# Turning the decayed k with VectorE and SBUF transfers in a gated-linear-attention and SiLU kernel

## The chip, the cores and the metric

The kernel runs on one core of a Trainium2 chip. The metric is the device time of one execution in microseconds (us), lower being better; it is the median of several runs. The core has five engines which work side by side, each through its own list of instructions: TensorE (PE in the profile; its weight loads are the row PEld), VectorE (DVE), ScalarE (ACT), GpSimd (POOL) and SyncE (SP), which here only issues transfers.

## The reference

Two blocks follow each other. Shapes: 4 batches, 8 heads, 768 tokens, 48 columns per head; then 3072 tokens of 384 columns through a hidden layer of 2048.

```python
def _attn_ref(q, k, v, alpha):
    state = np.zeros((B, H, D, D), dtype=np.float32)
    for t in range(S):
        state = alpha[:, :, t, :, None] * state + np.einsum('bhd,bhe->bhde', k[:, :, t], v[:, :, t])
        y[:, :, t] = np.einsum('bhd,bhde->bhe', q[:, :, t], state)
    return y

def _moe_ref(x, w_in, w_out):
    h = x @ w_in
    g = h * (1.0 / (1.0 + np.exp(-h)))
    return g @ w_out
```

Between them the heads are laid side by side, (B, H, S, D) to (B*S, H*D). The weights come as 64-bit floats, the rest as 32-bit floats.

## The kernel before, in words

The sequence is cut into 6 blocks of 128 tokens. A *chunk* n is one block of one batch, with all 8 heads: 24 chunks, the four batches of a block after each other (`ci, b = divmod(n, B)`). Heads lie in pairs: a tile of 128 partitions and 4 x 128 columns holds 4 pairs, each pair in two halves of 64 partitions of which 48 are used.

Within a chunk the recurrence is written with products of the decay. For each chunk there are five stages:

- `products(n)` takes the products of alpha backward over the chunk with a scan (L699), and multiplies k by them: `kp` (L713, L715). Up to chunk 7 (`NA` = 8) the inputs are brought to "column on partition" by TensorE transposes (L694); from chunk 8 on they are loaded in quads and turned by VectorE in blocks of 32x32 (`turned`, L674). From chunk 8 on, the two halves of 64 tokens of the heads of the second two pairs are swapped in `kp`.
- `quotient(n)` makes the forward products with a second scan (L728) and multiplies q by them (L733): `qp`.
- `scores(n)` multiplies `kp` with `qp` on TensorE (L757) into two PSUM banks, u = 0 and 1 for the two heads of a pair. Only the earlier tokens may count for a later one, so the result is masked: up to chunk 3 by a ScalarE copy and a GpSimd select (L763, L764), from chunk 4 on by a VectorE multiplication with a mask tile (L768). The masked scores are `g`. From chunk 8 on, the blocks of the scores that are zero anyway are not computed; `blank(n)` has ScalarE write zeros to the two banks ahead of time (L741). Then `kp` is transposed by TensorE (L774) and copied by ScalarE to `kn` (L776), with tokens on partitions; the last block of each batch (chunks 20 to 23) needs no `kn`. ScalarE also multiplies the state by the chunk's whole decay (L780).
- `values(n)` multiplies `g` with v, and the state with `qp`, on TensorE (L800) and copies the sum into `xt` (L805), the input of the second block.
- `states(n)` multiplies `kn` with v (L815) and adds that to the state on VectorE (L821), and after it v of chunk n+2 is loaded.

The second block works on groups of four chunks. Groups 0 and 1 multiply `xt` with `w_in` plainly (L858). The later ones save products by sums of blocks: `enter` (L882), with sums and differences on VectorE (L896) and copies and SiLU on ScalarE (L888, L893). `leave` multiplies with `w_out` in halves (L980), with subtractions on VectorE (L985) and stores of the result (L994, L996). The 64-bit weights are rounded to 32 bits on the way in: ScalarE takes the low part (L609, `rounding`), VectorE does the rest (L623 to L625); `convert` starts a piece at a time. In the second half an audit reads inputs again and VectorE reduces them (L663).

The order of the work is set on two levels. The loop over steps writes it: in step s, slot 0 has scores(s-1), slot 1 products(s), slot 2 values(s-1) and states(s-1), and slot 3, from step 8 on, quotient(s) and blank(s); `fill` puts pieces of the second block between the slots as their due times come. On this program the tile framework then works: it holds buffers in pools, adds the waits, and its planner may list instructions of an engine in another order than the one written, except where `keep_in_program_order` forbids it. On the chip each engine follows its list. The pool `ps_a` has three PSUM banks for scores, values, states and transposes; `kn`, `kp`, `qp` and `g` have one buffer each in the late steps. Nearly all transfers are issued on the sync queue, in the order of its list.

The change touches `scores`, `values`, `states` and `weights`, and puts `flip` in the place of `blank`:

Of the kernel before, what the change touches and what calls it, by code (L numbers as in the profile page):

```python
# [355 lines left out]
def quotients(  # L356
# [172 lines left out]

    mask = consts.tile([128, 2, C], F32, name="mask")  # L530
    gps.memset(mask, 1.0)
    for odd in range(2):
        for e in range(2):
            m = mask[CH * e : CH * e + CH, odd, :]
            gps.affine_select(m, m, pattern=[[1, C]], compare_op=ALU.is_ge, fill=0.0,
                              base=-CH * (e ^ odd), channel_multiplier=-1)

# [56 lines left out]
    def weights(which):  # L594
# [18 lines left out]
        for i, (dst, src) in enumerate(pieces):  # L613
            if not wide:
                act.dma_start(dst, src)
                yield
                continue
            assert which == 0 or conv_done[0] == n_conv[0]
            bits = coming.pop(0)
            up = ahead.pop() if ahead else rounding(bits)  # L620
            hi, w = bits[:, :, 1], dst.bitcast(I32)
            tc.keep_in_program_order(
                dve.tensor_scalar(w, hi, 3, 0x3FFFFFFF, ALU.logical_shift_left, ALU.bitwise_and))  # L623
            dve.scalar_tensor_tensor(w, hi, -(1 << 30), w, ALU.bitwise_and, ALU.bitwise_or)
            dve.tensor_tensor(w, w, up, ALU.add)  # L625
            if i + 1 < len(pieces):
                ahead.append(rounding(coming[0]))
            fetch()
            yield
# [104 lines left out]

    def blank(n):

        if n < NA:
            return
        ps = ctxs[n]["blank"] = [ps_attn() for _ in range(2)]
        for t in ps:  # L740
            act.activation(t.rearrange("p j c -> p (j c)"), ident[:, 0:1].to_broadcast([128, 4 * C]),  # L741
                           AF.Copy, scale=0.0)

    def scores(n):
        c = ctxs[n]
        ci, b = c["ci"], c["b"]
        ps = c.pop("blank") if n >= NA else [ps_attn() for _ in range(2)]

        for j in (0, 2, 1, 3):
            for e in range(2 if n >= NA else 1):
                for u in range(2):
# [4 lines left out]
                              start=True, stop=True)  # L758
        g = c["g"] = work.tile([128, 2, NP, C], F32, name="g")
        for u in range(2):  # L760
            if n < GB:

                act.copy(g[:, u], ps[u])  # L763
                gps.affine_select(g[:, u], g[:, u], pattern=[[0, NP], [1, C]], compare_op=ALU.is_ge,  # L764
                                  fill=0.0, base=0, channel_multiplier=-1)
                continue
            m = mask[:, :, None, :] if n >= NA else mask[:, 0:1, None, :]
            dve.tensor_tensor(g[:, u].rearrange("p (o j) c -> p o j c", o=2),  # L768
                              ps[u].rearrange("p (o j) c -> p o j c", o=2),
                              m.to_broadcast([128, 2, NP // 2, C]), ALU.mult)  # L770
        if ci < NCH - 1:
            ps_k = ps_attn()
            for j in range(NP):
                pe.transpose(ps_k[:, j, :], c["kp"][:, j, :], ident)  # L774
            c["kn"] = work.tile([128, NP, C], F32, name="kn")
            act.copy(c["kn"], ps_k)  # L776
# [8 lines left out]
    def values(n):  # L785

        c = ctxs[n]
        ci, b, g, qp = c["ci"], c["b"], c["g"], c["qp"]
        vn = c["v"].rearrange("p (j u) d -> p j (u d)", u=2)
        s = st[b].rearrange("p j u e -> p j (u e)")  # L790
        py = ps_attn()
        todo = [(3 * j + i, vn[:, j, at : at + 32], g[:, u, j, :])
                for j in range(NP) for i, at, u in ((0, 0, 0), (1, 32, 0), (2, 80, 1))]
        todo += [(3 * j + 1, vn[:, j, 48:80], g[:, 1, j, :]) for j in range(NP)]
        if ci > 0:
# [10 lines left out]
    def states(n):  # L806
        c = ctxs.pop(n)
        ci, b, vn = c["ci"], c["b"], c["v"]
        if ci < NCH - 1:

            ps = ps_attn()
            for j in range(NP):
                for i in range(4):
                    r = slice(32 * i, 32 * i + 32)
                    pe.matmul(ps[r, j, 0:D], lhsT=c["kn"][:, j, r], rhs=vn[:, 2 * j + i // 2, 0:D],  # L815
                              start=True, stop=True)
# [288 lines left out]
    def settle():  # L1105

        first.close()
        late.update(look=pool("look"), part=pool("part"), xc=pool("xc"), turn=pool("turn"),
                    wx=pool("wx").tile([128, 8, NQ, 128], F32, name="wx"))
        quads = pool("quads")  # L1110
# [5 lines left out]
    def fill(step, slot):  # L1116

        at = step * SLOTS + slot
        if at < marks[0]:
            if step >= 1:  # L1120
                convert(0, (at - SLOTS) * 3 // (marks[0] - SLOTS) + 1)
# [11 lines left out]
    for step in range(STEPS):  # L1133
# [6 lines left out]
        elif step >= NA:  # L1140
            stages = [[(scores, 1)], [(products, 0)], [(values, 1), (states, 1)], [(quotient, 0), (blank, 0)]]
        for slot, group in enumerate(stages):
            for stage, lag in group:
# [10 lines left out]
                if stage is states and n + NV < NT:  # L1154
                    load_v(n + NV)
            fill(step, slot)
            if step * SLOTS + slot >= NA * SLOTS - 1 and conv_done[1] == NFT and not late:
# [21 lines left out]
    ps = ps_attn()[0:1, 0, 0:1]  # L1179
    pe.matmul(ps, lhsT=good, rhs=mask[:, 0, C - 1 : C], start=True, stop=True)  # L1180
    dve.tensor_single_scalar(small, ps, 127.5, ALU.is_ge)
# [62 lines left out]
```

## Time and profile before

| | |
|---|---|
| time, median of 3 runs | 563.47 us (563.33 to 563.66) |
| span of the profiled execution | 561.6 us |
| busy PE, PEld | 543.9 us, 492.6 us |
| busy VectorE, ScalarE, GpSimd | 453.0, 205.3, 15.1 us |
| TensorE transposes of `kp`, L774 | 80 |
| ScalarE: blanks L741, copies of `kn` L776 | 32 of 0.598 us, 20 of 0.584 us |
| VectorE: masks L768 | 40 of 0.685 us |
| GpSimd: selects L764 | 8 of 0.865 us |

A line of groups gives the source line, engine, operation, output and inputs by name and shape, the count, the busy time and the mean duration of one. A fp32 matmul leaves two records, a transpose one, so the count of PE records is above that of the instructions. The slices cut the span in 40 and show the busy share of each in tenths. The chain is followed back from the last instruction to what released it, step by step, so it tells which engines' work set the end. Records of matmuls overlap, since they are pipelined: the distance between starts says what one costs, and their ends are modelled.

### The profile page before, as it was taken

How to read it: one execution, taken by the hardware profiler on the slowest of the kernel's cores; microseconds unless marked ns; L12 is line 12 of the kernel's file. 1: busy time of each engine (PE TensorE's matmuls, PEld its weight loads, DVE VectorE, ACT ScalarE, POOL GpSimd, SP SyncE). 2: the span in 40 equal slices, each digit the busy share in tenths (PEclk: the TensorE clock that was granted, in tenths of full speed). 3: DMA queues.
4: the chain of work that ended last, by engine and by line, in shares of the span. 5: the costliest groups of instructions: out<-in, count | busy, mean ns of one | idle time of the engine just before them, and what ended most of it. 6: DMA issues, size and time to landing. Idle time of an engine off the chain costs nothing.

```text
span 561.6 us, 12420 instructions
## 1 busy us (share of the span) xinstructions
PE 543.9 (97%) x5074; PEld 492.6 (88%) x5074; DVE 453.0 (81%) x829; ACT 205.3 (37%) x406; POOL 15.1 (3%) x36
## 2 busy tenths in 40 slices
PE   5899999999999999999999999999999999999996
PEld 3688887998999999899989999999998999899995
DVE  5797899966999799986998897899895875857731
ACT  2566543213233342443433443434443342332100
POOL 4211000100000000000000000000000000000000
PEclk9899999999999999999999999999999999999998
DMA  9989971143443333333425544435522123334200
GB/s 206 230 241 223 234 183 34 43 126 100 100 107 89 73 97 87 101 87 85 131 70 160 142 108 134 130 81 153 136 69 81 53 85 118 99 94 125 71 30 26
DMA packets 94417, 63.81 MB, mean 114 GB/s; under 512 B 55312, under 2 KB 86032, under 8 KB 94352
## 3 DMA queue, kind: packets, MB, share of 16 engines
q1 hardware_dynamic: 94352, 62.94, 43.3%
q8 instruction: 41, 0.67, 0.5%
q14 instruction: 24, 0.20, 0.1%
HBM read 58.20 MB, written 4.72 MB: 112 GB/s over the span
## 4 chain that ended last, share of the span: by engine, by line
PE 75%; DVE 14%; DMA 5%; SPq 2%; issue 2%; ACT 1%; POOL 0%; DVEq 0%; ACTq 0%
PE ps_o L980 33%; PE ps_m L882 18%; PE ps_m L858 11%; PE ps_a L800 6%; DMA bits<-in_moe_w_out_dram 3%; PE ps_a L757 3%; DVE seen L663 2%; PE ps_a L774 1%; DVE g L896 1%; DMA bits<-in_moe_w_in_dram 1%; DVE u L699 1%; PE ps_a L815 1%; DVE w_out L625 1%; DVE p L728 1%; SPq L456 1%
## 5 line engine op out<-in xcount | busy, mean ns | idle before, releaser
L980 PE MATMUL ps_o<-w_out,g 128*128 128x192 f32 x768 | 133.6, 328 | 1.1 <-DVE o L994 1.1
L980 PEld LDWEIGHTS ps_o<-w_out,g 128*128 128x128 f32 x768 | 125.5, 190 | 3.9 <-DVE o L994 1.5
L980 PE MATMUL ps_o<-wt,g 128*128 128x192 f32 x576 | 100.0, 327 | 0.0
L980 PEld LDWEIGHTS ps_o<-wt,g 128*128 128x128 f32 x576 | 95.1, 190 | 1.5
L858 PE MATMUL ps_m<-xt,w_in 128*128 128x256 f32 x384 | 88.5, 382 | 1.0 <-ACT xt L805 1.0
L858 PEld LDWEIGHTS ps_m<-xt,w_in 128*128 128x128 f32 x384 | 71.0, 190 | 11.0 <-ACT xt L805 1.4
L882 PE MATMUL ps_m<-xc,w_in 128*128 128x256 f32 x288 | 70.1, 379 | 0.0
L882 PEld LDWEIGHTS ps_m<-xc,w_in 128*128 128x128 f32 x288 | 54.0, 190 | 6.4 <-DVE g L896 0.2
L663 DVE TENSOR_REDUCE seen<-bits 128x1 f32<-128x384 int32 (+2 forms) x65 | 42.4, 689 | 16.8 <-DMA bits<-in_moe_w_out_dram 16.5
L893 ACT ACTIVATE g<-g 128x1024 f32<-128x1024 f32 x32 | 33.1, 1055 | 57.5 <-DVE g L896 57.5
L985 DVE TENSOR_TENSOR g<-g 128x512 f32<-128x512 f32 x72 | 48.5, 686 | 5.6 <-PE ps_o L980 5.6
L882 PE MATMUL ps_m<-xc,wx 128*128 128x256 f32 x192 | 50.1, 383 | 0.0
L888 ACT COPY g<-ps_m 128x512 f32<-128x512 f32 x64 | 36.8, 587 | 36.1 <-PE ps_m L882 36.0
L780 ACT ACTIVATE st<-st,least 128x96 f32<-128x96 f32 x80 | 24.1, 364 | 58.4 <-DVE least L702 58.4
L882 PEld LDWEIGHTS ps_m<-xc,wx 128*128 128x128 f32 x192 | 35.0, 190 | 4.2 <-issue 0.4
L896 DVE TENSOR_TENSOR g<-ps_m,g 128x512 f32<-128x512 f32 x56 | 37.4, 683 | 0.8 <-PE ps_m L882 0.5
L699 DVE TENSOR_TENSOR_SCAN u<-al,one 128x516 f32<-128x516 f32 x24 | 29.1, 1212 | 10.4 <-ACT al L696 10.3
L728 DVE TENSOR_TENSOR_SCAN p<-al,inv 128x516 f32<-128x516 f32 x24 | 29.4, 1226 | 5.2 <-PE ps_a L800 4.9
L861 ACT ACTIVATE g<-ps_m 128x512 f32<-128x512 f32 x32 | 19.0, 595 | 39.2 <-PE ps_m L858 39.0
L800 PE MATMUL ps_a<-g,vn 128*32 128x128 f32 x768 | 28.0, 282 | 3.9 <-POOL g L764 3.9
L800 PEld LDWEIGHTS ps_a<-g,vn 128*32 128x32 f32 x768 | 20.3, 112 | 11.2 <-issue 5.5
L768 DVE TENSOR_TENSOR g<-ps_a,mask 128x512 f32<-128x512 f32 x40 | 25.7, 685 | 4.0 <-PE ps_a L757 3.7
(125 smaller groups left out, 620.7 us busy)
## 6 DMA issues: line engine op xcount, KB each, us to landing
bits<-in_moe_w_in_dram SPq DMA_DIRECT2D x24, 512.0 KB, 4.7
bits<-in_moe_w_out_dram SPq DMA_DIRECT2D x32, 384.0 KB, 3.4
at<-in_alpha_dram SPq DMA_DIRECT2D x64, 96.0 KB, 2.4
kt<-in_k_dram SPq DMA_DIRECT2D x64, 96.0 KB, 2.6
qt<-in_q_dram SPq DMA_DIRECT2D x64, 96.0 KB, 2.5
bits<-in_alpha_dram SPq DMA_DIRECT2D x9, 512.0 KB, 3.8
out_dram<-o SPq DMA_DIRECT2D x48, 96.0 KB, 1.9
an<-in_alpha_dram SPq DMA_DIRECT2D x8, 192.0 KB, 5.1
```

Of the source, the lines that this page charges most:

```text
L663: dve.tensor_reduce(seen[kind][which][:, i : i + 1], x, axis=AX, op=op, apply_absolute_value=True))
L699: dve.tensor_tensor_scan(u[:, end - 1 :: -1], sg[:, end:0:-1], one[:, end:0:-1], 0.0, ALU.mult, ALU.add)
L728: dve.tensor_tensor_scan(p[:, 0:end], sg[:, 0:end], iv[:, 0:end], 0.0, ALU.mult, ALU.add)
L768: dve.tensor_tensor(g[:, u].rearrange("p (o j) c -> p o j c", o=2), ps[u].rearrange("p (o j) c -> p o j c", o=2), m.to_broadcast([128, 2, ...
L800: pe.matmul(py[32 * at : 32 * at + 32, t, :], lhsT=w, rhs=x, start=(i < 4), stop=(i >= len(todo) - 4), skip_group_check=True)
L858: pe.matmul(ps[:, e, :], lhsT=w_in[:, t, (f + e) * 128 : (f + e + 1) * 128], rhs=xt[:, t, :], start=(t == 0), stop=(t == NKT - 1))
L882: pe.matmul(ps[:, e], lhsT=block_w(w)[:, 2 * pair + e], rhs=block_x(grp, x), start=(first and e == 0), stop=(e == 1), skip_group_check=True)
L888: act.copy(to, ps)
L893: act.activation(x, x, AF.Silu)
L896: dve.tensor_tensor(to, a, b, op)
L980: pe.matmul(ps, lhsT=x, rhs=w[:, i], start=(first and i == 0), stop=(i == HF - 1), skip_group_check=True)
L985: dve.tensor_tensor(cells(grp, h, pair, *to), cells(grp, h, pair, *x), cells(grp, h, pair, *y), ALU.subtract)
```

## The change

The masked scores and the turned `kp` are made in another way from chunk 8 on.

- `kn` no longer comes from TensorE, PSUM and a ScalarE copy. `flip(n)`, in slot 3 after quotient, has VectorE transpose the 32x32 blocks of `kp`, and 16 transfers of 32 partitions x 128 columns on the sync queue carry the blocks to their partitions in `kn`. `states` reads it with its columns in another order.
- `blank` goes, and with it the zeros in PSUM and the mask tile. `g` becomes one fixed tile, `decayed`. From chunk 8 on ScalarE copies the computed blocks of the scores into it: per u one copy of 128 partitions and 256 columns and two of 64 partitions and 128 columns; four GpSimd selects of 64 partitions and 256 columns then clear what lies above the diagonal in place. The blocks never computed are cleared once, ahead of chunk 8.
- Chunks 4 to 7 mask as chunks 0 to 3 did: a copy and a GpSimd select per u.
- The first piece of `weights` stops once after its first `rounding`, so that the second rounding is written behind the first scores.

It is for taking the transposes off TensorE, the masks off VectorE and the zero writes off ScalarE, and for giving GpSimd a part.

```diff
-    mask = consts.tile([128, 2, C], F32, name="mask")
...
+    decayed = fix.tile([128, 2 * NP * C], F32, name="g")
+    low, high = slice(0, CH), slice(CH, C)
+    earlier, later = [(low, 0), (high, 1)], [(low, 1), (high, 0)]
...
             up = ahead.pop() if ahead else rounding(bits)
+            if which == i == 0:
+                yield
...
-    def blank(n):
...
+    def flip(n):
+        c = ctxs[n]
+        if n < NA or c["ci"] == NCH - 1:
+            return
+        t = late["flip"].tile([128, 4, NP, 32], F32, name="flip")
+        dve.transpose(t, c["kp"].rearrange("p j (c i) -> p c j i", i=32))
+        c["kn"] = work.tile([128, NP, C], F32, name="kn")
...
+        for r in range(4):
+            for i in range(4):
+                nc.sync.dma_start(kn[32 * i : 32 * i + 32, 128 * r : 128 * r + 128],
+                                  t[32 * r : 32 * r + 32, i, :])
...
     def scores(n):
-        ps = c.pop("blank") if n >= NA else [ps_attn() for _ in range(2)]
+        ps = [ps_attn() for _ in range(2)]
...
         for u in range(2):
-            if n < GB:
+            if n < NA:
                 act.copy(g[:, u], ps[u])
                 gps.affine_select(g[:, u], ...)
                 continue
-            dve.tensor_tensor(g[:, u]..., ps[u]..., m.to_broadcast(...), ALU.mult)
-        if ci < NCH - 1:
+            x = ps[u].rearrange("p (o j) c -> p o j c", o=2)
+            act.copy(swapped[:, :, u, :, CH:], x[:, :, :, CH:])
+            for r, o in earlier:
+                act.copy(swapped[r, o, u, :, 0:CH], x[r, o, :, 0:CH])
+        if n >= NA:
+            for at, half in ((0, earlier), (CH, later)):
+                for r, o in half:
+                    x = swapped[r, o].rearrange("p u j c -> p (u j) c")[:, :, at : at + CH]
+                    gps.affine_select(x, x, ...)
+        if n < NA and ci < NCH - 1:
             ps_k = ps_attn()
             for j in range(NP):
                 pe.transpose(ps_k[:, j, :], c["kp"][:, j, :], ident)
...
     def states(n):
+                    kn = c["kn"][:, j, r] if n < NA else c["kn"][:, i, 32 * j : 32 * j + 32]
...
-            stages = [..., [(values, 1), (states, 1)], [(quotient, 0), (blank, 0)]]
+            stages = [..., [(values, 1), (states, 1)], [(quotient, 0), (flip, 0)]]
```

## The prediction

> **What bounds the kernel now.** I read busy time and slices first.
>
> ```profile
> PE 543.9 (97%) x5074; PEld 492.6 (88%) x5074; DVE 453.0 (81%) x829; ACT 205.3 (37%) x406; POOL 15.1 (3%) x36
> PE   5899999999999999999999999999999999999996
> ```
>
> TensorE (PE) is busy 97%, and every slice but the first two and the last is at 9: what lengthens or opens a hole in its stream costs time in full. The chain that ended last agrees:
>
> ```profile
> PE 75%; DVE 14%; DMA 5%; SPq 2%; issue 2%; ACT 1%; POOL 0%; DVEq 0%; ACTq 0%
> ```
>
> Then the stretches of the late attention steps (start:end, length, busy PE, PEld, DVE, ACT, POOL):
>
> ```profile
> 300.00:340.00 40.00, 40.00 (x389) 36.85 (x378) 36.41 (x58) 17.91 (x35) 0.00 (x0) 1.00 0.50 136
> 340.00:380.00 40.00, 40.00 (x425) 36.67 (x424) 35.98 (x66) 14.09 (x25) 0.00 (x0) 1.00 0.37 99
> ```
>
> PE has no hole, and VectorE (DVE) is 36.4 of 40 busy: second in line, with 9% to spare. GpSimd does nothing here. Why PE has no hole shows in its timeline over one chunk (start, length):
>
> ```profile
> 308.50 0.90 PE L757 MATMUL ps_a<-p,kp 48*64 48x128 f32 x32
> 309.33 0.65 PE L774 MATMUL ps_a<-ident,kp 128*128 128x128 f32 x4
> 309.82 2.77 PE L980 MATMUL ps_o<-w_out,g 128*128 128x192 f32 x16
> ...
> 318.48 1.03 PE L882 MATMUL ps_m<-xt,w_in 128*128 128x256 f32 x4
> 319.44 1.08 PE L800 MATMUL ps_a<-g,vn 128*32 128x128 f32 x32
> 320.33 0.84 PE L800 MATMUL ps_a<-p,st 128*32 128x128 f32 x24
> 320.99 0.52 PE L815 MATMUL ps_a<-vn,kn 128*32 128x48 f32 x32
> ```
>
> Between scores (L757) and values (L800) stand 9.6 us of feed-forward matmuls, in which the mask is applied; values and states (L815) then follow without a wait. This filling is what I watch below.
>
> **What the skill says.** (1) "PSUM — Partial Sum Buffer", section Engine vs sequencer instructions: the queues of ScalarE, VectorE and GpSimd are strict FIFO, and matmuls start and complete in program order. The trace agrees: PE's records stand in the order in which its instructions were built, L757 to L815 above. So the built order of the changed kernel can be read as its execution order. (2) "VectorE: DVE Perf Modes", The three transpose paths: VectorE transposes 32x32 blocks only, so the blocks must be moved across partitions, which the 16 transfers do. The trace has the transpose at 1.11 us (L674). (3) "DMA: Bandwidth & Descriptors", Anatomy of one DMA: a transfer has some 2 us of fixed cost; here the 96 KB loads land after 2.4 to 2.6 us. (4) "SBUF — State Buffer", Who interferes with whom: a VectorE instruction with two SBUF inputs and a GpSimd instruction reading SBUF block each other. No late stretch has GpSimd work, so this trace can't show it.
>
> **Part by part.**
>
> *Removed from PE: the transposes L774 of 12 chunks (n = 8 to 19).* Chain with and without them (chunk 20 has none):
>
> ```profile
> 351.29 0.82 PE ps_a L757 x24
> 352.10 0.60 PE ps_a L774 x4
> 352.71 2.60 PE ps_o L980 x16
> ...
> 434.74 0.82 PE ps_a L757 x24
> 435.56 2.81 PE ps_o L980 x16
> ```
>
> 0.60 goes, but the next full-array group pays 0.21 for coming back from the small tiles: 0.39 x 12 = 4.7 us saved.
>
> *Early edits.* For n = 4 to 7 the masks leave VectorE (L768, 1.29 us for a pair); the chain runs through VectorE from 70 to 102 us and holds one such pair: 1.2 us. At the start scores end at 11.7, but ScalarE's copy (L763) starts only at 14.3, behind a rounding that waited for its load; PE waits 3.6 us for the result. Moved behind the scores, perhaps 1 to 2 us come back. Together 2.5 us. The extra copies and selects of n = 4 to 7 lie beside 2.6 us and more of matmuls.
>
> *Blanks, ps_k and its copy gone:* 32 x 0.598 (L741) and 12 x 0.584 (L776) of ScalarE, which is 37% busy: nothing. *VectorE late:* minus two masks (1.29), plus one transpose (1.0 to 1.1): even.
>
> *The new way to g.* L768 took 1.29 us for both halves. Now six copies and then four selects stand in a row. Copies: L805 gives 475 ns for 384 columns, L1010 317 for 192, so 0.82 ns a column; 256 columns 0.37, 128 columns 0.26; 2 x 0.37 + 4 x 0.26 = 1.8, less overlap (L763: two in 1.05 instead of 1.17) 1.5. Selects: 512 columns take 865 ns (L764), 128 columns 325 (four in 1.30, L535), so 256 about 0.43, four 1.7. Three hand-overs at 0.1: 3.3, I take 3.5 us from scores to values; bounds 2.5 and 4.5 (port conflicts of (4)).
>
> *The order.* The diff does not tell it: built, the changed kernel has another PE order. The framework's planner, which lists the instructions, seems to expect the 16 transfers late: states(n) now stand around scores and values of n+1, and it has pulled feed-forward work forward out of the gap. Full-array work between scores and values, counted from the built order (0.43 us per 256-column, 0.325 per 192-column matmul): before, 5.2 to 10.4 us for every late chunk. After, for n = 8 to 23: 5.2, 5.1, 2.1, 0, 2.2, 2.1, 1.3, 0, 1.7, 2.1, 0, 0, 1.3, 2.2, 5.2, 2.1. Against 3.5 us PE waits 1.4, 3.5, 1.3, 1.4, 2.2, 3.5, 1.8, 1.4, 3.5, 3.5, 2.2, 1.3, 1.4: **28.4 us**.
>
> *VectorE behind it.* Its states update (L821) of n-1 now waits for matmuls that stand after values(n), so VectorE stands still from the end of its transpose until then, scores 0.9 + 3.5 + values and states 2.1, less the transpose 1.1: 5.4 us a chunk, and it had 3.8 in 43 to spare. Behind the wait stand all products of the next chunk. Work from that update to the next scores, each operation at its step in the trace (transposes 0.95, scans 1.17, 512 columns 0.62, 256 columns 0.36, audit 1.12), against PE's work there: n=12 21.5 to 17.6; 14 17.8 to 12.5; 16 19.5 to 16; 18 18.6 to 12.1; 20 22.0 to 16.8; 13, 15, 17, 19, 21 PE is longer; 22 and 23 lose 1.6 each. Sum 3.9 + 5.3 + 3.5 + 6.5 + 5.2 + 3.2 = **27.6 us**.
>
> *Transfers.* An issue of such size takes 0.46 us on the sync queue (L465: four in 1.8), so 16 take 7.4. From the last states matmul: v and next loads (15 issues, 6.9), 7.4, landing 2.5: 16.8 us. PE comes to the last states matmuls after 11.7 (shortest gap) + 0.9 + 3.5 + 1.5 = 17.6 us: hidden, barely.
>
> *Single states matmuls* between full-array work: L815 x2 so placed cost 0.4 us each (61.68 to 61.88, and 2.79 for the next twelve instead of 2.59); some ten more, four groups merged, most inside waits: 2 us.
>
> Sum: 563.5 - 4.7 - 2.5 + 28.4 + 27.6 + 2 = 614; since copies may overlap more, I take **612 us**.
>
> **Rivals.** *A, faster:* g comes early enough everywhere and the order costs nothing: 563.5 - 4.7 - 2.5 = 556. For it: PE-bound stream, hidden mask. Against: PE starts in order, and four chunks have nothing between scores and values. *B, g waits alone:* VectorE keeps ahead; 563.5 + 28.4 - 7.2 + 2 = 587. For it: VectorE's waits overlap PE's. Against: 9% spare. *C, transfers rule:* issues cost twice (0.9; four of L465 once took 3.0) and audit fetches before them wait; kn lands near 25 us; five short gaps lose about 5 each: 635. For it: the sync queue already waits 72 us on L996. Against: 16 KB each.
>
> **Numbers.** Mine 0.56, B 0.19, C 0.14, A 0.11. Range 582 to 632: it holds mine, B and a part of C, and the ends of the g latency (13 chunks x 1 us each way); A and most of C are left out. Faster 0.11, same 0.01, slower 0.88.
>
> **What would show it.** Right: PE's waits for GpSimd's selects on the values line, 2 to 4 us each in a dozen chunks; VectorE waiting for the states matmuls, and PE's scores for VectorE's product; PE busy near 90%. C right: PE waiting for the kn transfers. Wrong if the select finishes within 2 us of the scores, or if PE has matmuls between the two lines.

## The result, and the profile after

| | before | after |
|---|---|---|
| time, median | 563.57 us (563.33 to 564.53, 4 runs) | 642.28 us (640.60 to 645.81, 4 runs) |
| ratio, 95% interval | | 1.140 (1.135 to 1.145) |
| span of the profiled execution | 561.6 us | 644.1 us |
| mean granted clock of TensorE | 0.994 | 0.956 |

Slower by 79 us, where 48 were predicted; the measured time lies above the range. The profile is of an execution of 645.8 us. Of e6 below, one execution in the slow state (1068 us at a granted clock of 0.79; with it the median would be 645.7) is left out. The granted clock is the share of its full speed at which TensorE was let run. The page of the changed kernel, busy times, slices, granted clock by slice, and the chain:

```profile
PE 577.8 (90%) x5026; PEld 506.5 (79%) x5026; DVE 444.7 (69%) x801; ACT 212.3 (33%) x466; POOL 47.5 (7%) x106
PE   6999999999997899698889967968997999999896
...
PEclk9999999999998999899699986969999899999999
...
PE 53%; DVE 17%; DMA 13%; SPq 6%; ACT 4%; issue 4%; POOL 2%; DVEq 0%; POOLq 0%; ACTq 0%
```

Read the first line against the one before: TensorE's idle time is 644.1 - 577.8 = 66.3 us, where it was 561.6 - 543.9 = 17.7. That is 48.6 of the 82.5 us by which the span grew. The other 33.9 are *busy* time, though 48 transposes fewer are done. So waiting explains little more than half, and why work got longer has to be asked as well. The slices say where both are: the holes lie in the late steps, and the clock is below 9 there and nowhere else. The chain runs in part through the issues of the new transfers (SPq, 4 of its 6% at L749), so they are one suspect; e6 below has none of them and is no faster.

The stretches that had no hole before:

```profile
300.00:340.00 40.00, 31.77 (x327) 24.97 (x326) 25.12 (x44) 14.88 (x32) 3.12 (x8) 0.83 0.32 77
340.00:380.00 40.00, 38.02 (x305) 33.59 (x300) 27.16 (x42) 12.11 (x28) 2.00 (x4) 1.00 0.52 122
```

VectorE (third of the busy times) fell from 36.4 and 36.0 to 25.1 and 27.2 of 40: second in line before, it now stands still a third of the time. The waits (engine, line, releaser: sum, times, longest):

```profile
PE ps_a L816 <- POOL g L785: 17.5, 11, 2.9
PE ps_m L899 <- DVE xc L561: 16.1, 5, 4.8
PE ps_m L899 <- DVE g L913: 9.6, 11, 1.5
PE ps_o L997 <- DVE o L1011: 6.4, 4, 2.6
...
PE ps_a L765 <- DVE p L734: 2.0, 2, 1.6
```

```profile
DVE st L838 <- PE ps_a L832: 47.6, 12, 8.6
```

Values (L816) wait for the selects, VectorE for the states matmuls (L832), and TensorE for VectorE in turn: much of the pattern that the prediction described. Nowhere does TensorE wait for kn. One chunk of it in TensorE's timeline, where 9.6 us of feed-forward matmuls lay between scores (now L765) and values:

```profile
301.05 0.27 PE L832 MATMUL ps_a<-vn,kn 128*32 128x48 f32 x2
301.25 0.90 PE L765 MATMUL ps_a<-p,kp 48*64 48x128 f32 x32
302.08 0.27 PE L832 MATMUL ps_a<-vn,kn 128*32 128x48 f32 x2
305.29 0.86 PE L816 MATMUL ps_a<-g,vn 128*32 128x128 f32 x10 [2.93 <-POOL g L785]
305.73 0.29 PE L832 MATMUL ps_a<-vn,kn 128*32 128x48 f32 x1
```

Scores are followed by nothing but single states matmuls of the chunk before, and 2.93 us of standing.

What the prediction did not have at all is the clock. Windows of 2 us (start:end, length, busy PE, PEld, DVE, ACT, POOL, clock) about the longest wait for a sum of VectorE (267.3 to 272.2):

```profile
266.00:268.00 2.00, 1.35 (x7) 0.84 (x5) 2.00 (x4) 0.58 (x3) 0.00 (x0) 1.00 0.11 25
268.00:270.00 2.00, 0.00 (x0) 0.00 (x0) 2.00 (x5) 0.73 (x1) 0.00 (x0) 1.00 0.11 25
270.00:272.00 2.00, 0.00 (x0) 0.00 (x0) 2.00 (x5) 1.20 (x2) 0.00 (x0) 0.51 0.12 27
272.00:274.00 2.00, 1.83 (x4) 1.51 (x5) 2.00 (x5) 1.13 (x2) 0.00 (x0) 0.50 0.38 113
274.00:276.00 2.00, 2.00 (x23) 1.23 (x24) 1.93 (x4) 0.00 (x0) 0.00 (x0) 0.50 0.19 49
276.00:278.00 2.00, 2.00 (x28) 1.59 (x24) 0.00 (x0) 0.47 (x2) 0.00 (x0) 0.78 0.04 8
```

TensorE pauses for 4.8 us, the clock goes to half during the pause and stays there for some 5 us of work after it. All nine pauses over 2.5 us in the late steps (2.6 to 4.8) have such a stretch in or after them. Their length alone does not decide, though. The stretches at half clock in the late steps last 3.41, 6.83, 10.24 or 13.65 us, once to four times 3.41, and all their edges lie on one grid of 3.41 us, in this profile and in every other one here that has more than one edge. In the changed kernel one step of the grid with 0.51 us of work is followed by one at half clock; in e1 (below) a pause of 3.24 us lies across an edge of the grid, each step keeps 1.7 us of work or more, and the clock stays at 1.00:

```profile
194.96:198.37 3.41, 0.51 (x18) 0.29 (x9) 0.71 (x1) 1.57 (x6) 1.56 (x4) 1.00 0.32 91
198.37:201.78 3.41, 3.38 (x76) 3.34 (x80) 0.00 (x0) 0.00 (x0) 0.00 (x0) 0.50 0.00 0
```

```profile
183.40:186.81 3.41, 1.89 (x62) 1.74 (x62) 3.38 (x7) 1.08 (x2) 0.00 (x0) 1.00 0.12 27
186.81:190.22 3.41, 1.70 (x34) 1.66 (x35) 1.97 (x4) 0.00 (x0) 0.00 (x0) 1.00 0.39 106
190.22:193.64 3.42, 3.42 (x20) 3.19 (x20) 1.71 (x5) 0.00 (x0) 0.00 (x0) 1.00 0.40 86
```

Counted over all 20 profiles, from steps at full clock: each of the 51 in which TensorE was idle for 2.03 us or more was followed by half clock, none of the 3112 with less than 1.45 us was, and 13 of the 40 between.

Summed over windows of 1 us, busy time times (1 - clock) is 20.7 us, 1.4 before: 19 of the 33.9 us of longer work. The rest can be read from the distances between starts, with the half clock taken out. The small matmuls of the late steps (scores, values, states) take 8 us more than before, 6.5 of it in states. The 256-column feed-forward matmuls take 8 us more, in part because the last one before a wait and the first one after it are longer. The transposes are 6 less, and 4 lie elsewhere.

### The profile page after: what moved, and what is told of

It reads as the page before. It is cut to its first block, busy times and chain, and to the rows that moved or that the text cites. A ratio compares the mean times of both kernels' runs of the same rounds, so it can differ in the third digit from the quotient of the medians.

```text
span 644.1 us, 12827 instructions
## 1 busy us (share of the span) xinstructions
PE 577.8 (90%) x5026; PEld 506.5 (79%) x5026; DVE 444.7 (69%) x801; ACT 212.3 (33%) x466; POOL 47.5 (7%) x106
## 4 chain that ended last, share of the span: by engine, by line
PE 53%; DVE 17%; DMA 13%; SPq 6%; ACT 4%; issue 4%; POOL 2%; DVEq 0%; POOLq 0%; ACTq 0%
PE ps_o L997 26%; PE ps_m L875 10%; DMA bits<-in_moe_w_out_dram 7%; PE ps_a L816 6%; SPq L749 4%; PE ps_m L899 4%; PE ps_a L765 3%; DVE g L913 3%; DVE seen L664 3%; POOL g L785 2%; DMA bits<-in_moe_w_in_dram 2%; ACT g L780 2%; PE ps_a L832 2%; DMA bits<-in_alpha_dram 1%; DVE turn L675 1%
## 5 line engine op out<-in xcount | busy, mean ns | idle before, releaser
L997 PE MATMUL ps_o<-w_out,g 128*128 128x192 f32 x768 | 137.1, 333 | 6.6 <-DVE o L1011 6.4
L997 PEld LDWEIGHTS ps_o<-w_out,g 128*128 128x128 f32 x768 | 127.8, 193 | 11.5 <-DVE o L1011 7.8
L899 PE MATMUL ps_m<-xc,w_in 128*128 128x256 f32 x288 | 79.4, 407 | 15.5 <-DVE xc L561 10.0
L875 PEld LDWEIGHTS ps_m<-xt,w_in 128*128 128x128 f32 x384 | 70.7, 190 | 11.5 <-ACT xt L821 1.6
L899 PE MATMUL ps_m<-xc,wx 128*128 128x256 f32 x192 | 54.9, 410 | 8.3 <-DVE xc L561 6.1
L1002 DVE TENSOR_TENSOR g<-g 128x512 f32<-128x512 f32 x72 | 48.3, 691 | 18.7 <-PE ps_o L997 18.4
L785 POOL TENSOR_SCALAR_AFFINE_SELECT g<-g 64x256 f32<-64x256 f32 x64 | 27.8, 456 | 373.1 <-ACT g L778 372.1
L905 ACT COPY g<-ps_m 128x512 f32<-128x512 f32 x64 | 36.4, 586 | 51.7 <-PE ps_m L899 43.2
L899 PEld LDWEIGHTS ps_m<-xc,wx 128*128 128x128 f32 x192 | 37.5, 204 | 16.1 <-DVE xc L561 6.5
L816 PE MATMUL ps_a<-g,vn 128*32 128x128 f32 x768 | 31.1, 297 | 17.9 <-POOL g L785 17.5
L838 DVE TENSOR_TENSOR st<-ps_a,st 48x192 f32<-48x192 f32 x32 | 11.3, 354 | 47.8 <-PE ps_a L832 47.6
L816 PEld LDWEIGHTS ps_a<-g,vn 128*32 128x32 f32 x768 | 22.7, 117 | 23.9 <-POOL g L785 19.8
L913 DVE TENSOR_TENSOR g<-ps_m,g 128x512 f32<-128x512 f32 x56 | 37.3, 681 | 1.0 <-PE ps_m L899 0.8
L913 DVE TENSOR_TENSOR g<-g,part 128x512 f32<-128x512 f32 x24 | 16.6, 694 | 21.7 <-ACT part L905 14.6
```

The source lines that it names most:

```text
L785: gps.affine_select(x, x, pattern=[[0, NP], [1, CH]], compare_op=ALU.is_ge, fill=0.0, base=0, channel_multiplier=-1)
L816: pe.matmul(py[32 * at : 32 * at + 32, t, :], lhsT=w, rhs=x, start=(i < 4), stop=(i >= len(todo) - 4), skip_group_check=True)
L875: pe.matmul(ps[:, e, :], lhsT=w_in[:, t, (f + e) * 128 : (f + e + 1) * 128], rhs=xt[:, t, :], start=(t == 0), stop=(t == NKT - 1))
L899: pe.matmul(ps[:, e], lhsT=block_w(w)[:, 2 * pair + e], rhs=block_x(grp, x), start=(first and e == 0), stop=(e == 1), skip_group_check=True)
L905: act.copy(to, ps)
L913: dve.tensor_tensor(to, a, b, op)
```

## The experiments

The theory T that I set out to test and its rivals C and G are named in the first expectation. "Order" is the order in which TensorE's instructions are built, and run; "old" is that of before, "torn" that of the changed kernel, "tied" that it was forced. One late chunk, with S scores, X transposes, G and T values, K states, numbers of calls, and F feed-forward work in us:

```
before:       S16 X4 F9.5 G16 T12 K16 F7.8
after:        S16 F0.4 K1 F1.7 K1 G16 T9 K13 T3 F12.1 K1     (K: of the chunk before)
```

The runs, by what they hold. Each ratio is to the kernel before, measured beside it.

| run | TensorE's order | kn by | time, us | ratio (95%) |
|---|---|---|---|---|
| changed kernel | torn | 16 transfers, sync queue | 642.3 | 1.140 (1.135 to 1.145) |
| e1 | old, tied | 16 transfers, sync queue | 613.6 | 1.089 (1.086 to 1.092) |
| e2 | old | TensorE | 561.9 | 0.995 (0.993 to 0.997) |
| e3: before + flip | torn | 16 transfers, sync queue | 635.7 | 1.130 (1.126 to 1.135) |
| e4: before + early edits | old | TensorE | 561.6 | 0.996 (0.994 to 0.998) |
| e5 | old | no transfer | 560.8 | 0.994 (0.992 to 0.996) |
| e6 | torn, tied | no transfer | 644.4 | 1.142 (1.139 to 1.144) |
| e7 | old | 16, GpSimd | 563.1 | 0.999 (0.998 to 1.000) |
| e8 | old | 16, ScalarE | 596.8 | 1.060 (1.057 to 1.063) |
| e9 | lumps torn, states in place | no transfer | 620.2 | 1.101 (1.098 to 1.105) |
| e10 | lumps in place, states late | no transfer | 597.8 | 1.062 (1.057 to 1.067) |
| e11: waits filled | torn, tied | 16, sync queue | 639.4 | 1.135 (1.131 to 1.138) |
| e12: e5, two p | old | no transfer | 557.9 | 0.990 (0.987 to 0.993) |
| e13: e7, two p | old | 16, GpSimd | 562.6 | 0.998 (0.997 to 0.999) |
| e14: e6, two p | torn, tied | no transfer | 633.3 | 1.123 (1.120 to 1.126) |
| e15: e1 | old, tied | 8 sync, 8 GpSimd | 574.6 | 1.020 (1.018 to 1.022) |
| e16: e1, two p | old, tied | 16, sync queue | 606.5 | 1.076 (1.073 to 1.078) |
| e17: e13, early order | old | 16, GpSimd | 561.7 | 0.996 (0.994 to 0.997) |
| e18: e17, kn unread | old | 16, GpSimd | 563.0 | 0.998 (0.997 to 0.999) |

### e1: the old order, all else changed

```diff
+    def in_order():          # called after each stage and each fill of the late steps
+        for i in (TensorE's instructions written since the last call):
+            tc.add_manual_dep(i, last.name, ...NoSync...)   # behind the one before, no wait
+            last = i
```

> The changed kernel, with TensorE's matmuls of the late steps tied to the order in which the source calls them: scores, 5.2 to 10.4 us of feed-forward matmuls, values, states, 5.2 to 7.8 us of feed-forward matmuls, as in the kernel before. Nothing else is changed: 12 x 16 transfers, copies and selects stay. Theory T (the planner's new order makes the stalls, and the stalls lower the clock): most of the loss is gone, 556 to 575 us, clock back near 0.99, PE's wait for the selects (17.5 us) and VectorE's for the states matmuls (47.6 us) nearly gone; a few us of PE waiting for kn remain in the chunks with short gaps (n = 9 to 11, 15.8 us from states to states against about 20 for 15 load issues, 16 transfer issues and a landing). Rival C (the transfers on the sync queue set the pace): states can no longer stand elsewhere, PE waits for kn 3 us or more in most of the 12 chunks, 595 us or more. Rival G (the copies and selects themselves are the cost): stays above 610.

613.6 us: not T's range. The time lies in C's, and in G's too, which e2 rules out. 29 us come back, 50 stay. The waits:

```profile
PE ps_a L832 <- DMA kn<-flip: 23.3, 12, 3.2
PE ps_o L997 <- DVE o L1011: 17.3, 5, 6.2
```

and in the sync queue's own timeline:

```profile
344.13 2.65 SPq L465 DMA_DIRECT2D qt<-in_q_dram  x4
346.83 11.05 SPq L749 DMA_DIRECT2D kn<-flip  x16
```

16 issues take 11.05 us, 0.69 each, behind loads that waited in the same queue. With the states in their old place kn is late in all 12 chunks, by 1.9 us on average where C said 3 or more. So rival C holds *for this order*: the planner had not moved the states for nothing. One thing is not as before here: VectorE's list still has the states update behind the flip of the next chunk.

### e2, e3, e4: the parts by themselves

```diff
 e2, from after:   -        if n < NA and ci < NCH - 1:      (transposes and copy for all n)
                   +        if ci < NCH - 1:
                   -  (quotient, 0), (flip, 0)
                   +  (quotient, 0)
 e3, from before:  + flip(n) and its 16 transfers, L774 and its copy for n < NA only
 e4, from before:  + copies and selects for n < NA, the yield in weights
```

> The changed kernel with kn made as before, by TensorE's four transposes and ScalarE's copy, so without VectorE's transpose and the 16 transfers; the masks by copies and selects and the early edits stay. The planned order is then that of the kernel before again. T: 559 to 564 us, since 5.2 us and more of matmuls stand between scores and values and hide the 3.1 us of copies and selects. C predicts the same, since the transfers are gone. Rival G (copies and selects cost by themselves, or GpSimd's reads hold VectorE up): 575 or more, with VectorE's operations beside the selects longer than in the kernel before.

> The kernel before with one part of the change: kn by VectorE's transpose and 16 transfers. Masks stay VectorE's multiplications, blanks and early steps stay. The planned order is as torn as the changed kernel's (states in single matmuls about scores and values, 11.7 to 21.2 us of feed-forward work in one lump before the scores). T and C: most of the loss is here already, 610 to 650 us, clock below 0.97. G: 575 or less.

> The kernel before with the early edits alone: copies and selects also for chunks 4 to 7, and the second rounding of the weights behind the first scores. My prediction's term: 2.5 us saved (1.2 from the mask pairs, 1 to 2 from the start), so 560 to 562 us. Rival: the chain through VectorE does not hold the masks and the start is set by the loads, so no difference (563.3 to 563.8).

All three as T expected. The copies and selects cost nothing while 5.2 us and more of matmuls stand behind the scores (561.9 against 561.6 for the early edits alone); the early edits save 0.42% (0.25 to 0.59), 2.4 us; the flip alone brings 71 of the 79 us.

### e5 and e6: the same two orders, without any transfer

```diff
-        t = late["flip"].tile([128, 4, NP, 32], F32, name="flip")
+        t = work.tile([128, 4, NP, 32], F32, name="kn")
...
+        c["kn"] = t                   # states read the blocks as they lie; no dma_start
...
 e6 only:
+    order = (the position of each of TensorE's 2577 calls in the changed kernel's list)
+    for a, b in zip(order, order[1:]):
+        tc.add_manual_dep(b, a.name, ...NoSync...)
```

Both leave out the transfers, so their states are not the reference's; the work and its shapes stay.

> The changed kernel without its 16 transfers: states read VectorE's transposed blocks as they lie, so the states are not the reference's; VectorE's transpose, copies, selects and early edits stay. The planned order of TensorE is then by itself that of the kernel before. After the first four runs (order kept with the transfers 613.6, kn by TensorE 561.9) I expect: if the transfers and what they do to the order are the whole loss, 556 to 561 us (4.7 for the transposes on top of the early edits, less what PE pays when it comes back from small tiles). If VectorE's transpose is a cost of its own (0.7 us in each chunk's chain of products), 565 or more.

> The kernel of the run before (no transfers, states not the reference's), with TensorE's matmuls tied to the order that they have in the changed kernel, one by one. This is the order's cost without any transfer. If order and transfers add up (613.6 less 560 for the transfers, 642 less 613.6 for the order): 585 to 595 us. If my prediction's working is right (28 of waits for the selects and 28 of scores waiting for VectorE, from the order alone): 610 or more, with the clock at 0.97 or below. If the order only costs where late transfers meet it: 560 to 572.

This pair settles the first question. Without one transfer of kn on the chip the torn order costs 644.4 - 560.8 = 84 us, as much as the whole change; TensorE's waits are like the changed kernel's:

```profile
PE ps_a L816 <- POOL g L785: 18.7, 12, 2.9
PE ps_m L899 <- DVE g L913: 14.6, 5, 6.5
PE ps_m L899 <- DVE xc L561: 11.9, 5, 4.7
```

The clock is 0.954. VectorE's own waits are shared out otherwise, at the second scan, which waits for values (0.9 us in the changed kernel), and at the states update (47.6 there):

```profile
DVE p L729 <- PE ps_a L816: 41.3, 6, 9.8
DVE st L838 <- PE ps_a L832: 22.7, 7, 8.2
```

So it may be partly chance that the totals agree so closely. With two p buffers in both orders, where the wait at the scan is gone, the order costs 633.3 - 557.9 = 75 us (e14 and e12, below). So transfers and order do *not* add up: with the old order the transfers cost 53 us (613.6 to 560.8), with the torn order nothing (642.3 to 644.4), since the torn order is just what hides them.

### e7 and e8: another engine issues the transfers

```diff
-                nc.sync.dma_start(kn[32 * i : ...
+                gps.dma_start(kn[32 * i : ...          (e8: act.dma_start)
```

> The changed kernel with its 192 transfers issued by GpSimd instead of the sync queue, all else as it is. The planned order of TensorE is then by itself that of the kernel before. If what costs is the sync queue's issue time (16 x 0.6 us on top of 15 loads, stores and audit fetches, each of which can wait): kn comes in time and the run takes 556 to 575 us. If the transfers themselves are slow to land or disturb TensorE's reads: 600 or more, as in the run with the order kept. A third way: GpSimd's own issues take 1 us or more each and push back its selects, which stand behind them: PE waits for the selects in the chunks with 5.2 us between scores and values, 575 to 600.

> The same with ScalarE issuing the 192 transfers. Sync queue as cause: the wait for kn goes as with GpSimd, but ScalarE, at 35%, carries 10 us more in each of 12 chunks and its copies and Silu stand behind VectorE's transpose: 565 to 595 us, with TensorE waiting for ScalarE's copies instead. Transfers themselves as cause: 600 or more.

In both the planner leaves the old order by itself. GpSimd, idle before, issues one in 0.50 us, and the loss is gone: 563.1. The transfers as such cost little, 2.3 us over e5; it was the queue they stood in. ScalarE (596.8, just above what was expected) is the wrong place: its copies and SiLU stand in line behind its own issues, which wait:

```profile
ACT g L878 <- DMA kn<-flip: 26.6, 4, 11.9
...
ACT g L905 <- DMA kn<-flip: 21.2, 4, 6.5
```

### e9 and e10: the torn order in two halves

Same tie as in e6, with mixed lists: `S16 F2.2 G16 T12 K16 F12.1` (e9) and `S16 K2 F9.5 G16 T9 K13 T3 K1 F7.8` (e10).

> No transfers (states not the reference's), TensorE's matmuls tied to a mixed order: feed-forward work as in the changed kernel (0 to 5.2 us of it between scores and values, 11.7 to 21.7 us in one lump behind), but the 16 states matmuls of a chunk whole, right behind its values. It separates the two halves of my prediction's working. By that working only the waits for the selects are left: 560.8 + 28.4 = 589, or about 580 with the 17.5 us that the changed kernel's trace has of them, and 5 to 10 more for the clock. If the late states are what costs (VectorE held up): below 575. If the lumps of feed-forward work alone cost everything: 630 or more.

> The other half: no transfers (states not the reference's), feed-forward work in its old place (5.2 to 10.4 us between scores and values), the states matmuls where the changed kernel has them relative to scores and values: single ones about the next chunk's scores, 13 behind its values. By my prediction's working VectorE's states update then waits a chunk longer, with all products of the next chunk behind it: 560.8 + 27.6 and the single matmuls, 590 or more. If the feed-forward lumps are what costs: 575 or less.

Both runs lose, 59 and 37 us over e5. In e9, where no states are late, TensorE waits for more than the selects, and the time is 30 us above the 589 of the prediction's working:

```profile
PE ps_a L816 <- POOL g L785: 20.7, 11, 3.1
PE ps_m L899 <- DVE g L913: 10.3, 7, 4.5
PE ps_m L899 <- DVE xc L561: 9.1, 5, 3.3
```

A lump of 12 to 22 us of feed-forward needs VectorE's sums (L561, L913) while VectorE works through the products, which it could not begin before values: its wait for them (scan L729) is 33.2 us in sum. The lumps thus make TensorE wait twice, with the clock (0.974) on top. e10 is less clean than meant:

```profile
PE ps_a L832 <- DVE kn L743: 25.6, 10, 3.6
```

The wait is for VectorE's transpose, whose single tile the late states hold; in the changed kernel the transfers free that tile. It is more than all the idle time that e10 has over e5 (39.7 to 19.1 us). So e10 does not show what late states cost through waits in the changed kernel. What carries over is the longer work of the small matmuls, 7 us over e5, where e9 has none.

### e11: the waits filled with useless work

```diff
         py = ps_attn()
+        for _ in range({10: 3, 11: 7, 12: 2, ...}.get(n, 0)):      # 52 in all
+            pe.matmul(py[...][:, 0:256], lhsT=w_in[:, 0, 0:128], rhs=w_in[:, 1, 0:256], start=True, stop=True)
```

> The changed kernel, transfers and all, with TensorE tied to the order it has, and 52 full matmuls (128x256, nobody reads their result) put ahead of values in 13 chunks, so many that each wait for the selects is filled with work: 22 us of work in place of 17.5 us of waiting. If waits only cost their length, 642 to 650 us. If the pauses also make the chip grant TensorE a lower clock for microseconds afterwards (clock 0.956; five of the eight stretches at half clock begin with a wait of 2.8 to 2.9 us for the selects): less time with more work, 625 to 638, clock above 0.965.

639.4 us, between the two expected ranges. 22 us more work take no more time, though the 17.5 us of waits that they replace are shorter; the clock is 0.981 instead of 0.956, and (1 - clock) x span is 12 us instead of 28. TensorE's busy time grew by 12.7 us only (590.5 to 577.8), not 22: the rest ran faster. The waits for VectorE's sums (15.7 for L561) and VectorE's own remain, so little of it reaches the end. That pauses lower the clock is shown; that all 19 us of it would come back without them is not.

### e12 to e14, e17, e18: where the saved transposes went

```diff
-    qps = [(spare if i else fix).tile(...) for i in range(2)]       # one p in the late steps
+    qps = [fix.tile(...) for i in range(2)]
...
-        p = turns(qps, n)
+        p = qps[(n + 1) % 2]
 e13, e16, e17, e18:
+    u3 = u1                                        (768 B, for room)
 e17, e18:
+        tc.keep_in_program_order(t)                (chunk 8's transposes in `turned`)
 e18:
+        c["kn"] = t                                 (the transfers fill a tile that nobody reads)
```

> The run without transfers (560.8; states not the reference's) with a second buffer for the decayed q (p), so that VectorE's second scan need not wait for the values of the chunk before. In that run TensorE has 3.9 us less to do between the first and the last of the late scores than with the transposes, but takes as long: it waits for VectorE's product p. If the single buffer of p is what makes VectorE late, the 4.7 us of the transposes come out now: 556 to 558. If VectorE's load is: 560 to 561.5, unchanged.

> A whole kernel that may beat both: the changed kernel with its transfers issued by GpSimd and a second buffer for p; the 2 KB for it come in part from computing the sum u3 in the place of u1. The transfers through GpSimd alone gave 563.1 against 563.8, and the second p took the run without transfers from 560.8 to 557.9. If the two add: 558 to 561 us, below the kernel before and below the run with the early edits alone (561.6). If GpSimd's transfers (0.50 us each) push back its selects and eat the gain: 561 to 564.

> The torn order without transfers (645.7; states not the reference's), with a second buffer for p. In the torn order VectorE's second scan waits 41 us for values, since p is still read by them. If that wait is what turns the order into lost time: 615 us or less. If the time is lost because feed-forward lumps need VectorE's sums just when it still works through the products, whatever the buffer: 635 or more. My prediction's working (VectorE stands still for the late states) says the second: 635 or more.

> The kernel with GpSimd's transfers and two p buffers (562.6), with VectorE's first late transposes (chunk 8) held in the place where the source has them. In that run the planner had put them some 20 chunk-us early, among the conversions of the weights; TensorE then stood 1.95 us for the states update at 99.6 us, its clock fell for a stretch (0.91 between 100 and 120 us) and the first late scores came at 135.3 us, against 131.2 in the run without transfers that has two p buffers. If this is all that ate the gain: 558 to 560 us. If GpSimd's transfers cost in the late stage: 561 or more.

In e5 TensorE is busy 540.6 us, 5.7 less than in e4, but the time is the same within 1 us, since it waits for VectorE's product:

```profile
PE ps_a L765 <- DVE p L734: 3.5, 4, 1.0
```

With two p this is gone and the gain comes out (557.9). In the torn order (e14) the second p brings 11 of 84 us: it is a part, not the cause. In the whole kernel it does not come out (562.6; 561.7 with the early loss mended). The states in one chunk of e12 and then of e17:

```profile
231.19 0.52 PE L832 MATMUL ps_a<-vn,kn 128*32 128x48 f32 x32
```

```profile
231.88 0.92 PE L834 MATMUL ps_a<-vn,kn 128*32 128x48 f32 x32
```

In the built program of e17 the first four states matmuls of a chunk wait for four transfers each, 16 completions in all. The profile shows no standing there, yet the group is 0.40 us longer (0.25 to 0.29 in e7). It does show eight semaphore instructions of 0.051 us at each of the 12 groups (0.41 us a group):

```profile
L834 PEldq EVENT_SEMAPHORE  x96: 51/51/51, 138.3 to 360.8; - x96
```

One more run has the transfers without these waits:

> The run e17 (GpSimd's transfers, two p buffers, 561.7 us), with all transfers made, but into a tile that nobody reads: states take VectorE's blocks as they lie, so the states are not the reference's, and TensorE has no transfer to wait for. It tells what costs the 0.25 to 0.40 us by which the states group of a chunk is longer with the transfers (0.92 against 0.52). If it is the 16 completions that the first four states matmuls check: the group is back at 0.52 and the run takes 557.5 to 559.5 us. If it is the transfers themselves, beside TensorE's reads: 561 to 562.5, group still above 0.7.

Half of this came true. The group is back at its old length:

```profile
232.57 0.52 PE L834 MATMUL ps_a<-vn,flip 128*32 128x48 f32 x32
```

and of the 96 semaphore instructions 4 are left, so the 16 checks cost, not the transfers; a chunk's transposes had been priced at 0.39. But the time is 563.0, not 558. From the first late scores to the last, e12 takes 297.5 us, e17 300.4 and e18 298.8: 1.6 come back, and 2.3 go into one wait for selects that stand behind GpSimd's transfers. The rest of the difference lies ahead of that, where no edit was meant to act: the first late scores come at 131.2 us in e12 and e17, 132.7 in e18, 135.3 in e13. Why the early part scatters so from build to build is not settled. So no kernel with the states of the reference came out better than the early edits alone: e2, e4 and e17, 0.995 to 0.996, cannot be told apart.

### e15 and e16: what makes kn late in the old order

```diff
 e15:
-                nc.sync.dma_start(kn[32 * i : ...
+                (nc.sync if i % 2 else gps).dma_start(kn[32 * i : ...
 e16:  two p buffers as above
```

> The run with TensorE's order kept (613.6) with 8 of the 16 transfers of a chunk issued by GpSimd, 8 by the sync queue. If the sync queue's time for issuing them (0.6 us each) is what makes kn late: 5 us a chunk come back, about 12 x 4 = 48, 563 to 575 us. If it is only the place of the transfers in the sync queue, behind v, loads and audits, whatever their number: 600 or more.

> The run with TensorE's order kept and all transfers on the sync queue (613.6), with a second buffer for p (and u3 in the place of u1). The loop states, v and next loads, 16 transfers, kn, states stays closed through the sync queue. If that loop sets the pace, little changes: 600 to 614 us. If VectorE's wait for values (single p) sets when the transposes and so the transfers start: 585 or less.

Half the issues, and 39 of the 50 us come back; the wait for kn falls from 23.3 us to:

```profile
PE ps_a L832 <- DMA kn<-flip: 2.8, 3, 1.0
```

So the number of issues on the sync queue is the main cause. VectorE's earlier start (e16) brings 7: the wait for kn halves (11.5 us), but TensorE's wait for VectorE's output sums o, 17.3 us in e1, is 19.9 here (6.8 in e15). Where that wait comes from was not followed.

## Why the prediction was right in direction and wrong in size

Right: that the built order, not the operations, decides, and in the main which waits TensorE has. e6 shows it without any transfer. Wrong: the size, 48 for 79 us. The steps that failed are two: the lower clock after pauses, put at nothing (19 us), and the matmuls that get longer, put at 2 us (8 for the small ones, and 8 for feed-forward matmuls beside waits). The waits themselves, 56 in the prediction, came out near (idle time +48.6), though not where they were put. By its terms:

- *Transposes, -4.7.* TensorE's busy time does fall (5.7 us, e5 to e4), but nothing of it reached the time: first VectorE's product was the next limit (single p), and with the transfers 16 checks in the states group (e17, e18) give 0.25 to 0.40 us a chunk back. The step failed that let a saving on the busiest engine count in full.
- *Early edits, -2.5.* Measured alone 2.4 (1.4 to 3.3). The first late scores come at 132.07 us instead of 133.96.
- *Waits for g, +28.4.* 17.5. The path takes 3.1 us (scores' end 335.0 to values 338.1) to 3.6, not 3.5: copies 1.6, selects four in 1.6. Over the 13 chunks that takes 3.6 off. Another 5.9 are filled by what stands in the gap beside the feed-forward work that was counted: single states matmuls, and feed-forward matmuls that take longer next to them. 1.3 are a wait for VectorE in the gap of chunk 20.
- *VectorE behind it, +27.6.* 16.1 + 9.6 + 6.4 + 2.0 = 34.1, but not where it was put: 2.0 at the scores, the rest at feed-forward matmuls that wait for VectorE's sums. I had taken the pulled-forward feed-forward work as always ready; e9 shows it isn't.
- *Single states matmuls, +2.* The term most off in proportion: 8. Some ten at 0.4 us were priced. One takes 0.2 us from its start to the next one's (301.05 to 301.25 above; 16 in a row take 0.45), but the built order has 48 groups of late states where there were 12, and 72 changes between the small groups (S, G, T, K) where the order of e5 has 28. With the half clock taken out, the small late matmuls take 8 us more in e6 than in e5, 7 in e10, and nothing in e9, whose states stand whole.
- *Clock, not in the sum.* 19 us of longer work. The Trainium skill has it: "TensorE: Matmul & The Clock Gate", Part 1: The HAM clock gate, says that TensorE's clock falls to half after about 3.4 us of idling and comes back after about as much sustained work, and its section HAM oscillation names loops that pause for that long. The prediction counted waits of 3.5 us in a dozen chunks and didn't ask for this. Here less idling was enough: 2.03 us within one step of the 3.41 us grid always, less than 1.45 never. So pauses of 2.6 to 2.9 us brought the clock down where they left enough idle time in one step, and one of 3.24 us that was shared between two steps (e1) did not. The stretches at half clock were 3.4 to 13.7 us long, the longer ones where pauses followed each other.
- *Feed-forward matmuls beside waits, not in the sum.* 8 us, read from the distances between starts. e9, with the lumps alone, has 5 of it over e5, and e10, with the late states alone, none.
- *Transfers hidden, "barely".* In the torn order true (no wait for kn). With the old order it was wrong: an issue took 0.59 to 0.69 us, not 0.46, so 10 to 11 us for a chunk's 16; my sum of 16.8 us becomes 6.9 + 11.05 (e1) + 1.8 = 19.8. The rival that transfers rule (C) is the other face of it.

The sum that fits: idle +48.6 (56 predicted), clock 19, small matmuls 8, feed-forward matmuls 8, transposes -6, elsewhere 4; about 82 of the 82.5 us of span. The chance for A, 0.11, was for "the order costs nothing"; e7 shows that this kernel existed one word away, at 563.

What is open: how the early part comes to differ by 1 to 4 us between builds; why the planner expects transfers from the sync queue so much later than the same ones from GpSimd or ScalarE (seen only in what it builds), what TensorE's wait for o in e1 and e16 comes from, and what late states cost through waits when no single tile holds VectorE up as in e10.

## What to carry to other kernels

When a change gives a planner a new long-latency step, compare the built order of the busiest engine first: the order can cost far more than the operations, and moving the step to another queue may give the old order back. A pause of TensorE can cost more than its length, for the clock that follows it: here from some 1.5 to 2 us of idle time within one step of 3.41 us on, so that where a pause falls counts as well as how long it is. A saving on the busiest engine is worth nothing until the engine that is second, and the waits that the new way adds on the busiest one, have been looked at.

## What the runs showed of the hardware that I had not expected

- A transfer of 16 KB within SBUF took the sync queue 0.59 us (median in the changed kernel) to 0.69 us (a chunk of e1) to issue and GpSimd 0.50 us; it landed after 1.8 us (sync) and 2.6 us (GpSimd).
- Checks of completed transfers are not free on TensorE: 16 on four matmuls, with eight semaphore instructions of 0.051 us, took 0.25 to 0.41 us (groups of 0.52 us grew to 0.77 to 0.93 in e7, e13 and e17).
- VectorE's 32x32 transpose of 128x512 fp32 took 0.71 us in the flip and 1.1 us in `turned`; the two differ in the order in which elements are read and written, and nothing else was tried.
- A single states matmul among other matmuls took 0.2 us from its start to the next start; 16 in a row took 0.45 us together.
- The granted clock changed only at steps of a 3.41 us grid, and it fell when TensorE had been idle for 2.03 us or more within one step (51 of 51 cases).
- The mutual blocking taken from "SBUF — State Buffer", Who interferes with whom, shows only weakly: in e2 four selects took 1.77 us in one chunk and 2.56 in the one before, beside VectorE's transposes and scans (mean of one 0.51 us, 0.46 in the changed kernel, where VectorE stands still more), and VectorE's subtractions (L1002) took 0.700 us between 200 and 420 us, 0.680 in e4. Matmuls covered all of it.
